# First batch of a spectral MLP kernel: filter rows, store queue and load order

## The chip, the cores and the metric

The kernel runs on one core of one Trainium2 chip. The metric is the device time of one execution in microseconds (us), the median of the runs shown. The engines are TensorE (PE, with its weight loads PEld), VectorE (DVE), ScalarE (ACT), GpSimd (POOL) and SyncE (SP), which here only issues DMAs; ACT can issue DMAs too. An engine takes its instructions in order, a DMA issue included.

## The reference

A batch of 4 sequences of 3136 tokens with 256 features goes through three parts. In the reference's words, cut:

```python
X = np.fft.rfft(x, axis=1)
y = np.fft.irfft(X * (filt_r + 1j * filt_i)[None], n=3136, axis=1)      # part 1: a filter per frequency and feature
u = y + np.real(np.fft.fft(np.fft.fft(y, axis=1), axis=2))              # part 2: mixing, then an MLP
x2 = u + np.maximum(layer_norm(u) @ w_ch1, 0) @ w_ch2
out = x2 + np.maximum(layer_norm(x2) * g_ln @ v_ch1, 0) @ v_ch2         # part 3: a second MLP
```

The weights are float64 and are handed to the kernel as pairs of 32-bit words; everything else is float32. The MLPs have 1024 hidden features.

## The kernel before, in words

The sequence length is 64 x 49, and a transform over it is done as one of length 64 (over p) and one of length 49 (over q), each a matrix product with a constant matrix.

For a batch b, `over_p(b)` loads x in 13 chunks (256 KB each, the last one 128 KB), multiplies each by the matrix `f1`, copies the product from PSUM to a buffer `gst` on ACT and stores it to the DRAM tensor `g` (tile `gd`). `over_q(b)` reloads g in 16 chunks with the axes exchanged (`gr`, 98 rows of 2 KB) and goes through 17 steps t. A step multiplies by `f2` (and by a turned copy `f2s`), multiplies the spectrum by a chunk of the filter (`fc`) on DVE, adds the two parts into y on POOL (line 423), multiplies y by `i1` two steps later, and stores the result to the DRAM tensor `v` (`vd`, 100 rows of 2 KB, issued by ACT). The filter input `ff` has 128 rows per frequency, of which rows 0 to 48 and 64 to 112 hold the filter and the other 30 are zero.

For batch 0 these products are single float32 ones; for later batches operands are split into a high and a low part. After batch 0's `over_q`, `prep_ticks(0)` mixes and normalises the first block, and the MLP steps (`w1_step`, `w2_step`) run until the end, with the stages of the next batches interleaved.

The weight words are loaded in chunks of 512 KB (`ww`) and converted to two float32r parts by `conv_ticks`: four DVE passes, two ACT passes, a multiplication on POOL and a split on ACT and POOL for each chunk. The conversion is a generator; each tick handles a different phase of up to four chunks. The first three chunks of the first weight have a generator of their own (`cv`, letter `a`).

The order of the work is written out by hand. The order in which the program emits instructions is the order on each engine. Tables say after which tick of which stage a tick of something else is emitted: `DURING` by the tick of `over_q(0)`, `P0` by the tick of `over_p(0)`, `AFTER` behind `over_q(0)`. The letters are `a` and `c` (conversion ticks), `k` (load of constants), `s` (split of constants), `x` (loads of x of batch 1), `f` (tick of `over_p(1)`) and `p` (tick of `prep_ticks(0)`). DMAs of SP and ACT use eight completion counters in turn: a DMA waits until the earlier one on the same counter has landed.

In the kernel before, SP's queue for batch 0 begins with the first constant, seven chunks of x, two chunks of words, six chunks of x, five further constants, the thirteen stores of g, and only then the first filter chunk, a constant, a chunk of words and the reloads of g:

```python
            (nc.sync if exact(k) else nc.scalar).dma_start(out=pairs(g_dram[b][k * 256:k * 256 + n * 128]), in_=st[:, :n])
```

Of the kernel before, what the change touches and what calls it, by code (L numbers as in the profile page):

```python
# [9 lines left out]
F32 = mybir.dt.float32  # L10
# [3 lines left out]
ACTF = mybir.ActivationFunctionType  # L14
# [4 lines left out]
B, S, D, H = 4, 3136, 256, 1024  # L19
# [14 lines left out]
NCONST = len(CN) * 128 + 2 + NK + D + 128  # L34
# [94 lines left out]
NA, LAG = 3, 3  # L129
N1 = 8  # L130
AHEAD, XW = 4, 7
WHEN = (-1, -1, 0, 1, 3, 3, 4, 5)
DURING = {0: 'aa', 2: 'a', 6: 'a', 14: 'k', 16: 'a', 30: 'cs', 33: 'x', 35: 'ff', 36: 'sf', 37: 'cc', 39: 'f', 40: 'f'}
P0 = {9: 'a'}
AFTER = "ppcfspfcppfpfppfpppc"
CONV = (0, 1, 3, 6, 9, 11, 12, 14, 15, 17, 19, 20, 21, 22, 23, 24, 25, 26, 27, 28)
P1 = (2, 3, 4, 5, 7, 8, 9, 10, 10)
# [11 lines left out]
def spectral_mlp_kernel(ctx: ExitStack, tc, x, ff, cst, w1a, w2a, gln, w1b, w2b, out):  # L149
    nc = tc.nc  # L150
# [7 lines left out]
    wp = pool("wp", 1)  # L158
# [7 lines left out]
    fp = pool("fp", 3)  # L166
    tp = pool("tp", 1)
    yp = pool("yp", 3)
    zp2 = pool("zp2", 3)
    stg = pool("stg", 3)  # L170
    up = pool("up", 3)
    xnp = pool("xnp", 5)
# [25 lines left out]
    g_sb = keep.tile([128, 2], F32, name="g_sb")  # L198
    zsl = {s: keep.tile([128, 2, B, 64], F32R, name=f"zsl{s}") for s in "hl"}
    alt = keep.tile([128, D], F32R, name="alt")  # L200
    zmid = keep.tile([128, 256], F32R, name="zmid")
# [36 lines left out]
    g_dram, v_dram, zt_of = {}, {}, {}  # L238
    x_raw, x_tile = {}, {}
    g_raw = {}  # L240
    f_sb, f_tile = {}, {}
# [5 lines left out]
    def load_x(b, c):  # L247
        if b > 1 or c > 9 or (c > 3 if b else c < 4):
            t = raw.tile([128, 2, D], F32, tag="raw", name="xr")
        else:  # L250
            if c % 2 == 0:
                x_tile[0] = up.tile([128, 4, D], F32, tag="u", name="xr")
            t = x_tile[0][:, c % 2 * 2:c % 2 * 2 + 2]
        n = blocks_of(c)
        nc.sync.dma_start(out=t[:, :n], in_=x[b, :, 2 * c:2 * c + n])
        x_raw[b, c] = t[:, :n]

    def pairs(t):
        return t.rearrange("(j p) d -> p j d", p=128)
# [3 lines left out]
    def load_g(b, c):  # L263
# [2 lines left out]
        nc.sync.dma_start(out=t[:98], in_=src)  # L266
        g_raw[b, c] = t[:98]

    def load_f(b, i, eng=nc.sync):
        k0, k1 = XCH[i]  # L270
        nk = k1 - k0
        if b == 0 and i > 2:
            if i < 5:
                t = up.tile([128, 4, D], F32, tag="u", name="fc").rearrange("p a d -> p (a d)")
            else:
                j = i - 5
                if j % 4 == 0:
                    f_tile[0] = wp.tile([128, 4096], F32, tag="w" + ("2a", "1b", "2b")[j // 4], name="fc")
                t = f_tile[0][:, j % 4 * 1024:j % 4 * 1024 + 1024]
            t = t.rearrange("p (a t d) -> p a t d", t=2, d=D)  # L280
            eng.dma_start(out=t[:, :nk], in_=ff[:, k0:k1])
            f_sb[b, i] = t[:, :, 0], t[:, :, 1]
        else:
            t = fp.tile([128, 2, 2, D], F32, tag="f", name="fc")
            eng.dma_start(out=t[:, :nk], in_=ff[:, k0:k1])
            f_sb[b, i] = t[:, :, 0], t[:, :, 1]
# [19 lines left out]
    def over_p(b):  # L306
        g_dram[b] = dram.tile([NJ * 128, D], F32, tag="g", name="gd")
        NC = 13
        for c in range(3):
            if (b, c) not in x_raw:  # L310
                load_x(b, c)
        yield

        def exact(c):
            return b == 0 or b == 1 and c < N1

        xs = {c: operand(exact(c), x_raw.pop((b, c))) for c in range(2)}
        yield
        done = []

        def store():
            k, n, ps = done.pop()
            if b == 0 and k % 5 > 2:
                st = vrp.tile([128, 2, D], F32, tag="vr", name="gst")
            elif b == 1 and exact(k):
                if k % 2:
                    st = tp.tile([128, 2, D], F32, tag="t2", name="gst")
                else:
                    st = hp.tile([128, 512], F32R, tag="hl", name="gst").bitcast(F32)
                    st = st.rearrange("p (a d) -> p a d", d=D)  # L330
            else:
                st = stg.tile([128, 2, D], F32, tag="st", name="gst")
            nc.scalar.activation(out=st[:, :n], in_=ps[:, :n], func=ACTF.Copy)  # L333
            (nc.sync if exact(k) else nc.scalar).dma_start(out=pairs(g_dram[b][k * 256:k * 256 + n * 128]), in_=st[:, :n])

        for c in range(NC):
            if c + 3 < NC and (b, c + 3) not in x_raw:
                load_x(b, c + 3)
            if b == 1 and c == N1:
                for i in range(c, c + 2):  # L340
                    xs[i] = operand(False, x_raw.pop((b, i)))
                yield
            if c + 2 < NC and not (b == 1 and N1 - 2 <= c < N1):
                xs[c + 2] = operand(exact(c + 2), x_raw.pop((b, c + 2)))
            n = blocks_of(c)
            ps = bank(2)
            product(exact(c), ps[:, :n].rearrange("p a d -> p (a d)"), "f1", xs.pop(c), 0, n * D)
            if done:
                store()
            done.append((c, n, ps))  # L350
            if b > 1 or c == NC - 1 or not exact(c + 1):
                store()
            yield

    def over_q(b):
# [4 lines left out]
        n = len(XCH)  # L360
# [18 lines left out]
        for c in range(3):  # L379
            load_g(b, c)  # L380
        if b == 0:
            for i in range(1, ahead):
                load_f(b, i)
        yield
        gs[0] = operand(b == 0, g_raw.pop((b, 0)))
# [103 lines left out]
    def load_v(U):  # L489
        ts = []  # L490
        for eo in range(2):
            t = vrp.tile([128, 2, D], F32, tag="vr", name="vr")
            r0 = 50 * 32 * eo
            if U < NU:
                r0 += 64 * (1 + U % 6 * 4)
                nc.sync.dma_start(out=t, in_=pairs(v_dram[U // 6][r0:r0 + 256]))
            else:
                for b in range(B):
                    h = 64 * (b % 2)
                    nc.sync.dma_start(out=t[h:h + 64, b // 2], in_=v_dram[b][r0:r0 + 64])  # L500
            ts.append(t)
        v_raw[U] = ts
# [211 lines left out]
    def run(it, k=None):  # L714

        while it and (k is None or k > 0):
            if next(it, StopIteration) is StopIteration:
                return False
            if k is not None:
                k -= 1  # L720
        return True

    with tc.manual_schedule():
        def load_consts(c0, c1):
            if c0 % 512 == 0:
                i = c0 // 512
                t = hp.tile([128, 512], F32R, tag="h" + "hhl"[i], name="cr").bitcast(F32)
                cf[i] = t
            t = cf[c0 // 512][:, c0 % 512:c0 % 512 + c1 - c0]
            nc.sync.dma_start(out=t, in_=cst[:, c0:c1])  # L730
            return t

        def consts():
            for i in (2, 1, 0):
                cs_done.add(i)
                split(cf[i], chi[:, i * 512:i * 512 + 512], clo[:, i * 512:i * 512 + 512],
                      nc.vector if i == 2 else nc.gpsimd)
                yield
# [9 lines left out]
        def bufs_b(kind, i):  # L748
# [9 lines left out]
                return flat(yp.tile([128, 2, D], F32, tag="y", name="wm"))  # L758
            return flat(zp2.tile([128, 2, D], F32, tag="z", name="we"))

        load_consts(0, 128)
        p0 = over_p(0)
        for c in range(XW):
            load_x(0, c)
        cv = conv_ticks(["1a"], bufs_a, lambda i: -1 if i < 2 else 1, 0, NA)
        run(cv, 1)
        for c in range(XW, 13):
            load_x(0, c)
        run(p0, 1)
        load_consts(128, 512)  # L770
        nc.sync.dma_start(out=ctail, in_=cst[:, nw - 128:nw - 128 + ctail.shape[1]])
        nc.sync.dma_start(out=g_sb, in_=gln)
        ar = zp2.tile([128, 2, D], F32, tag="z", name="ar")[:, 0]
        nc.sync.dma_start(out=ar, in_=cst[:, NCONST - D - 128:NCONST - 128])
        turned[0] = xnp.tile([128, D], F32, tag="xn", name="f2s")[:, :128]
        nc.sync.dma_start(out=turned[0], in_=cst[:, NCONST - 128:])
        cs = consts()
        q0 = over_q(0)
        k = 0
        while run(p0, 1):  # L780
            k += 1
            for what in P0.get(k, ""):
                run(cv, 1)
        load_f(0, 0)
        load_consts(512, 1024)
        for what in DURING.get(0, ""):
            run(cv, 1)
        nc.scalar.activation(out=alt, in_=ar, func=ACTF.Copy)
        nc.scalar.activation(out=zmid, in_=ar, func=ACTF.Copy, scale=0.0)
        p1 = over_p(1)  # L790
        act = {
            "a": lambda: run(cv, 1),
# [8 lines left out]
        k = 0  # L801
        while run(q0, 1):
            k += 1
            for what in DURING.get(k, ""):
                act[what]()
        load_v(0)
        p = prep_ticks(0)
        for what in AFTER:
            act[what]()
# [2 lines left out]
        nc_ = sum(v.count("c") for v in (*DURING.values(), AFTER))  # L812
        assert nf >= 2 + N1
        assert sum(v.count("s") for v in (*DURING.values(), AFTER)) == 3
        assert sum(v.count("a") for v in DURING.values()) + sum(map(len, P0.values())) >= NA + LAG


        blocks = [(0, 0)]
# [156 lines left out]
```

## Time and profile before

| what | value |
|---|---|
| median of 3 runs | 1425.43 us (1424.55 to 1427.17) |
| the profiled execution | 1426.04 us, its span 1424.3 us |
| PE busy | 1382.0 us, 97% of the span |
| DVE, ACT, POOL busy | 62%, 44%, 29% |
| DMA | 123.66 MB, 87 GB/s over the span |

The page gives shares over the whole span. They hide that the kernel has two parts: a beginning of some 160 us in which the engines wait for each other and for transfers, and the rest, in which PE has no pause. The views that show the beginning are the windows (busy time by stretch), the timeline of one engine, the chain of waits and the list of DMA issues.

### The profile page before, as it was taken

What the parts mean: (1) busy time and instruction counts of PE and PEld (TensorE: products, weight loads), DVE (VectorE), ACT (ScalarE), POOL (GpSimd) and SP (SyncE); (2) the same over time, 40 slices, a digit from 0 to 9 for tenths busy, and PEclk for the clock granted to TensorE, in tenths of its full rate; (3) what the DMA queues carried; (4) which work ended last, traced back from release to release, by engine and by line L of the source; (5) the groups of instructions that cost most, each with busy time, mean ns of one, the idle gap of its engine ahead of it and who ended that gap; (6) DMA issues with size and microseconds to landing.
All of it is one profiled execution on the core that took longest, in us unless ns stands there. A gap on an engine that the chain in (4) does not pass through costs nothing.

```text
span 1424.3 us, 22897 instructions
## 1 busy us (share of the span) xinstructions
PE 1382.0 (97%) x8835; PEld 1218.7 (86%) x8835; DVE 879.4 (62%) x1798; ACT 622.7 (44%) x1350; POOL 408.4 (29%) x361
## 2 busy tenths in 40 slices
PE   4968999999999999999999999999999999999998
PEld 2437899888989999898999998898999999999998
DVE  1779977777554765766544676667555555555453
ACT  4655545546444444545344355445333233323222
POOL 1636534544231333434032244334100010100000
PEclk7999999999999999999999999999999999999999
DMA  9983332422233313312233223131000000000000
GB/s 322 305 286 108 103 113 69 140 92 71 79 117 121 97 53 109 110 46 68 71 104 114 83 85 114 48 109 62 19 30 30 31 1 31 31 16 16 31 15 23
DMA packets 65981, 123.66 MB, mean 87 GB/s; under 512 B 6096, under 2 KB 32848, under 8 KB 65872
## 3 DMA queue, kind: packets, MB, share of 16 engines
q1 hardware_dynamic: 49920, 99.00, 21.3%
q10 hardware_dynamic: 15952, 23.20, 5.0%
q8 instruction: 69, 1.13, 0.3%
q14 instruction: 40, 0.33, 0.1%
HBM read 83.12 MB, written 39.06 MB: 86 GB/s over the span
## 4 chain that ended last, share of the span: by engine, by line
PE 90%; DMA 4%; DVE 3%; ACT 1%; issue 1%; POOL 1%; SPq 0%; ACTq 0%; POOLq 0%
PE ps L705 37%; PE ps L682 37%; PE ps L217 11%; PE ps L612 3%; DMA xr<-in_x 2%; PE ps L303 1%; DMA vd<-vst 1%; DMA fc<-in_ff 1%; PE ps L440 1%; DVE we L652 1%; ACT gst L333 0%; DVE wm L665 0%; DMA gd<-gst 0%; PE ps L550 0%; DVE hl L688 0%
## 5 line engine op out<-in xcount | busy, mean ns | idle before, releaser
L687 ACT ACTIVATE hh<-ps 128x512 fp32r<-128x512 f32 (+1 forms) x400 | 235.6, 589 | 686.5 <-PE ps L682 664.8
L688 DVE SCALAR_TENSOR_TENSOR hl<-ps,hh 128x512 fp32r<-128x512 f32 (+1 forms) x400 | 271.7, 679 | 426.1 <-ACT hh L687 425.0
L682 PE MATMUL ps<-xth,w1a 128*128 128x512 f32 (+1 forms) x800 | 245.6, 389 | 0.0
L682 PE MATMUL ps<-xth,w1b 128*128 128x512 f32 (+1 forms) x800 | 243.7, 386 | 0.0
L705 PE MATMUL ps<-w2a,hh 128*128 128x256 f32 x1568 | 221.3, 283 | 1.3 <-ACT hh L687 1.3
L705 PE MATMUL ps<-w2b,hh 128*128 128x256 f32 x1568 | 218.3, 281 | 0.0
L705 PEld LDWEIGHTS ps<-w2b,hh 128*128 128x128 f32 x1568 | 206.2, 188 | 10.5
L705 PEld LDWEIGHTS ps<-w2a,hh 128*128 128x128 f32 x1568 | 205.2, 189 | 10.3 <-ACT hh L687 2.0
L599 POOL TENSOR_TENSOR rs<-rs,mhalf 128x4 f32<-128x4 f32 (+1 forms) x51 | 50.4, 988 | 415.8 <-DVE rs L598 407.5
L682 PE MATMUL ps<-xtl,w1a 128*128 128x512 f32 (+1 forms) x400 | 155.9, 390 | 0.0
L682 PE MATMUL ps<-xtl,w1b 128*128 128x512 f32 (+1 forms) x400 | 155.7, 389 | 0.0
L682 PEld LDWEIGHTS ps<-xth,w1a 128*128 128x128 f32 x800 | 135.9, 189 | 17.8 <-ACT xth L220 0.5
L682 PEld LDWEIGHTS ps<-xth,w1b 128*128 128x128 f32 x800 | 135.1, 188 | 16.5
L705 PE MATMUL ps<-w2a,hl 128*128 128x256 f32 x784 | 122.9, 278 | 3.5 <-DVE hl L688 3.5
L705 PE MATMUL ps<-w2b,hl 128*128 128x256 f32 x784 | 121.9, 277 | 0.0
L423 POOL TENSOR_TENSOR y<-y,t 128x512 f32<-128x512 f32 (+1 forms) x67 | 87.0, 1299 | 101.6 <-DVE t L421 85.9
L705 PEld LDWEIGHTS ps<-w2a,hl 128*128 128x128 f32 x784 | 104.5, 188 | 4.1 <-DVE hl L688 4.1
L705 PEld LDWEIGHTS ps<-w2b,hl 128*128 128x128 f32 x784 | 103.8, 188 | 0.0
L221 POOL TENSOR_TENSOR sl<-gr,sh 98x512 fp32r<-98x512 f32 x48 | 63.3, 1319 | 109.5 <-ACT sh L220 109.5
L221 POOL TENSOR_TENSOR sl<-y,sh 128x512 fp32r<-128x512 f32 (+1 forms) x51 | 67.1, 1316 | 80.3 <-issue 59.4
L682 PEld LDWEIGHTS ps<-xtl,w1a 128*128 128x128 f32 x400 | 75.3, 188 | 14.9
L682 PEld LDWEIGHTS ps<-xtl,w1b 128*128 128x128 f32 x400 | 75.2, 188 | 14.4
(114 smaller groups left out, 2030.1 us busy)
## 6 DMA issues: line engine op xcount, KB each, us to landing
fc<-in_ff SPq DMA_DIRECT2D x61, 512.0 KB
vd<-vst ACTq DMA_DIRECT2D x64, 200.0 KB
gr<-gd SPq DMA_DIRECT2D x64, 196.0 KB
xr<-in_x SPq DMA_DIRECT2D x48, 256.0 KB
vr<-vd SPq DMA_DIRECT2D x48, 256.0 KB
out<-u SPq DMA_DIRECT2D x24, 512.0 KB
gd<-gst ACTq DMA_DIRECT2D x28, 256.0 KB
gd<-gst SPq DMA_DIRECT2D x20, 256.0 KB
```

The source lines that it names most:

```text
L217: nc.tensor.matmul(out=o, lhsT=lhs[a], rhs=rhs[b], start=start and i == 0, stop=stop and i == 2)
L221: (lo_eng or nc.vector).tensor_tensor(out=lo, in0=src, in1=f32(hi), op=ALU.subtract)
L303: nc.tensor.matmul(out=o, lhsT=cf[i // 512][:k, i % 512:i % 512 + w], rhs=rhs[:k, c0:c1], start=start, stop=stop)
L423: (nc.gpsimd if b or t < n - 1 else nc.vector).tensor_tensor(out=y[:, :nk], in0=y[:, :nk], in1=t2[:, :nk], op=ALU.add)
L440: nc.tensor.transpose(zp[:, a].rearrange("p t k -> p (t k)"), z[:, a], ident)
L599: nc.gpsimd.tensor_tensor(out=rs[:, tl], in0=rs[:, tl], in1=mhalf[:, tl], op=ALU.pow)
L612: nc.tensor.transpose(ps[:, t * 128:t * 128 + 128], xs[t][:, k * 128:k * 128 + 128], ident)
L652: nc.vector.scalar_tensor_tensor(out=p, in0=w[:, :, 1], scalar=-0x80000000, in1=p, op0=ALU.bitwise_and, op1=ALU.bitwise_or)
L682: nc.tensor.matmul(out=ps[:, :n], lhsT=w[:, a, k, m * 128:m * 128 + 128], rhs=xt[s][:, k, :n], start=i == 0, stop=i == 5)
L687: nc.scalar.activation(out=h[:, :n], in_=ps[:, :n], func=ACTF.Relu)
L688: nc.vector.scalar_tensor_tensor(out=l[:, :n], in0=ps[:, :n], scalar=0.0, in1=f32(h[:, :n]), op0=ALU.max, op1=ALU.subtract)
L705: nc.tensor.matmul(out=o[:, t % 2], lhsT=a[:, t * 128:t * 128 + 128], rhs=w[:, b, m], start=m == 0 and i == 0 and t % 2 == 0, stop=m == 7 ...
```

## The change

- The filter chunks of batch 0 are loaded in three DMAs each: rows 0 to 47, rows 64 to 111, and the two rows 48 and 112. Rows 32 to 63 and 96 to 127 of the place are cleared before, by POOL, or by DVE for the first two of the three large places. All large places are allocated at the beginning and each filter chunk keeps the place it had.
- The stores of g for batch 0 are issued by ACT, each behind its copy.
- The order on SP is now: first constant, all x, constants, filter chunks 0 and 1, a constant, the reloads of g, filter chunks 2 and 3, and then a chunk of words at a time. The conversion of the first three chunks of words runs wholly within `over_q(0)`. Two small inputs (`ar`, `gln`) are loaded at its eighth tick, and the two ACT copies of `ar` come after it.

The diff, cut to its core:

```diff
-DURING = {0: 'aa', 2: 'a', 6: 'a', 14: 'k', 16: 'a', 30: 'cs', 33: 'x', 35: 'ff', 36: 'sf', 37: 'cc', 39: 'f', 40: 'f'}
-P0 = {9: 'a'}
+DURING = {2: 'a', 7: 'a', 12: 'a', 15: 'a', 18: 'a', 19: 'k', 22: 'a', 26: 'a', 29: 'cs', 32: 'x', 34: 'ff', 35: 'sf', 36: 'cc', 38: 'f', 39: 'f'}
...
+    def rest(t, eng):
+        for r in (32, 96):
+            eng.memset(t[r:r + 32], 0.0)
+
+    def rows(t, src):
+        for r in (slice(0, 48), slice(64, 112), slice(48, 113, 64)):
+            nc.sync.dma_start(out=t[r], in_=src[r])
...
             if i < 5:
                 t = up.tile([128, 4, D], F32, tag="u", name="fc").rearrange("p a d -> p (a d)")
+                rest(t, nc.gpsimd)
             else:
                 j = i - 5
-                if j % 4 == 0:
-                    f_tile[0] = wp.tile([128, 4096], F32, tag="w" + ("2a", "1b", "2b")[j // 4], name="fc")
-                t = f_tile[0][:, j % 4 * 1024:j % 4 * 1024 + 1024]
+                t = f_tile[j // 4][:, j % 4 * 1024:j % 4 * 1024 + 1024]
             t = t.rearrange("p (a t d) -> p a t d", t=2, d=D)
-            eng.dma_start(out=t[:, :nk], in_=ff[:, k0:k1])
+            rows(t[:, :nk], ff[:, k0:k1])
+            f_sb[b, i] = t[:, :, 0], t[:, :, 1]
+        elif b == 0:
+            t = fp.tile([128, 2, 2, D], F32, tag="f", name="fc")
+            rest(t.rearrange("p a t d -> p (a t d)"), nc.gpsimd)
+            rows(t[:, :nk], ff[:, k0:k1])
             f_sb[b, i] = t[:, :, 0], t[:, :, 1]
...
-            (nc.sync if exact(k) else nc.scalar).dma_start(out=pairs(g_dram[b][k * 256:k * 256 + n * 128]), in_=st[:, :n])
+            (nc.sync if b and exact(k) else nc.scalar).dma_start(out=pairs(g_dram[b][k * 256:k * 256 + n * 128]), in_=st[:, :n])
...
-            for i in range(1, ahead):
+            for i in range(2, ahead):
                 load_f(b, i)
...
         load_consts(0, 128)
         p0 = over_p(0)
-        for c in range(XW):
+        for c in range(13):
             load_x(0, c)
-        cv = conv_ticks(["1a"], bufs_a, lambda i: -1 if i < 2 else 1, 0, NA)
-        run(cv, 1)
-        for c in range(XW, 13):
-            load_x(0, c)
+        for j, n in enumerate(("2a", "1b", "2b")):
+            f_tile[j] = wp.tile([128, 4096], F32, tag="w" + n, name="fc")
+            if j < 2:
+                rest(f_tile[j], nc.vector)
         run(p0, 1)
...
+        load_f(0, 0)
+        load_f(0, 1)
+        load_consts(512, 1024)
         cs = consts()
         q0 = over_q(0)
...
+        run(p0)
+        run(q0, 1)
+        rest(f_tile[2], nc.gpsimd)
+        cv = conv_ticks(["1a"], bufs_a, lambda i: i - 1, 0, NA)
...
         while run(q0, 1):
             k += 1
+            if k == 8:
+                ar = xnp.tile([128, D], F32, tag="xn", name="ar")
+                nc.sync.dma_start(out=ar, in_=cst[:, NCONST - D - 128:NCONST - 128])
+                nc.sync.dma_start(out=g_sb, in_=gln)
             for what in DURING.get(k, ""):
                 act[what]()
         load_v(0)
+        nc.scalar.activation(out=alt, in_=ar, func=ACTF.Copy)
+        nc.scalar.activation(out=zmid, in_=ar, func=ACTF.Copy, scale=0.0)
```

SP's queue between the loads of x and the reloads of g, before (`gst` are the copies to be stored to g, `cr` constants, `fc` filter chunks, `ww` weight words, `gr` reloads of g; line numbers are those of the kernel before):

```order
L334 DMA gd<-gst 128x2x256 x12
L334 DMA gd<-gst 128x256
L285 DMA fc<-in_ff 128x1024
L730 DMA cr<-in_cst 128x512
L637 DMA ww<-in_w1a 128x1024
L266 DMA gr<-gd 98x512 x3
L285 DMA fc<-in_ff 128x512
L285 DMA fc<-in_ff 128x1024
```

The same place now, up to the fourth reload of g (line numbers of the changed kernel; `f2s` is the turned matrix):

```order
L786 DMA f2s<-in_cst 128x128
L275 DMA fc<-in_ff 48x1024 x2
L275 DMA fc<-in_ff 2x1024
L275 DMA fc<-in_ff 48x512 x2
L275 DMA fc<-in_ff 2x512
L742 DMA cr<-in_cst 128x512
L265 DMA gr<-gd 98x512 x3
```

The thirteen stores have left SP's queue, and the reloads of g stand behind the first two filter chunks and a constant; the chunk of words comes after filter chunk 3, three filter DMAs for each chunk.

POOL's queue from its first work to the first additions y of the stage over q, before:

```order
L203 MEMSET mhalf 128x4
L654 ISA
L654 TENSOR_TENSOR we<-we 128x512
L221 TENSOR_TENSOR w1a<-we,w1a 128x512
L654 TENSOR_TENSOR we<-we 128x512
L423 TENSOR_TENSOR y<-y,t_284 128x512
L423 TENSOR_TENSOR y<-y,t_295 128x256
```

And now:

```order
L202 MEMSET mhalf 128x4
L271 MEMSET fc 32x1024 x8
L271 MEMSET fc 32x4096 x2
L435 ISA
L435 TENSOR_TENSOR y<-y,t_270 128x512
L271 MEMSET fc 32x1024 x2
L435 TENSOR_TENSOR y<-y,t_287 128x256
```

Ten clears stand before the first addition, and the two clears of filter chunk 4 (the fifth) between the first and the second.

## Rows read from the trace of the kernel before

**Rows 1.** Windows: each engine's busy time (instructions), granted clock, DMA share, GB/s.
```profile
core 0: us, PE busy (x) PEld busy (x) DVE busy (x) ACT busy (x) POOL busy (x), PEclk, DMA share, GB/s
0.00:10.00 10.00, 5.77 (x7) 2.49 (x8) 0.00 (x0) 2.75 (x4) 0.30 (x5) 1.00 0.76 255
10.00:20.00 10.00, 7.95 (x20) 3.42 (x18) 2.82 (x6) 3.49 (x7) 0.00 (x0) 1.00 1.06 374
20.00:30.00 10.00, 0.00 (x0) 0.00 (x0) 0.69 (x1) 6.70 (x14) 1.47 (x2) 0.50 1.01 334
...
50.00:60.00 10.00, 10.00 (x30) 4.50 (x29) 7.25 (x12) 7.44 (x22) 5.58 (x4) 1.00 0.89 282
60.00:70.00 10.00, 10.00 (x29) 4.52 (x28) 6.33 (x11) 7.62 (x24) 5.75 (x4) 1.00 0.98 349
70.00:80.00 10.00, 9.41 (x26) 3.91 (x25) 5.61 (x10) 6.64 (x20) 4.32 (x3) 1.00 0.93 324
...
110.00:160.00 50.00, 45.04 (x276) 39.45 (x275) 45.78 (x76) 29.27 (x59) 28.89 (x23) 0.97 0.33 111
160.00:1424.00 1264.00, 1257.95 (x8350) 1141.61 (x8347) 771.41 (x1614) 531.92 (x1139) 339.81 (x302) 1.00 0.21 67
```

**Rows 2.** Timeline of PE: start, duration, instruction, [idle before, what ended it].
```profile
4.23 13.71 PE L303 MATMUL ps<-xr,cr 128*128 128x512 f32 x26 [4.23 <-DMA xr<-in_x]
32.39 4.60 PE L303 MATMUL ps<-gr,cr 98*128 98x256 f32 x8 [14.45 <-DMA fc<-in_ff]
...
41.74 1.02 PE L303 MATMUL ps<-gr,cr 98*128 98x512 f32 x2
...
78.45 1.02 PE L409 MATMUL ps<-gr,f2s 98*128 98x512 f32 x2
...
107.52 1.63 PE L682 MATMUL ps<-xth,w1a 128*128 128x512 f32 x2
```

**Rows 3.** Timeline of ACT, 0 to 46 us.
```profile
17.89 5.04 ACT L333 ACTIVATE gst<-ps 128x512 f32<-128x512 f32 x8 [5.75 <-DMA gd<-gst]
...
24.90 0.40 ACT L788 ACTIVATE alt<-ar 128x256 fp32r<-128x256 f32 x1
```

**Rows 4.** The chain of waits: start, duration, what it went through.
```profile
14.78 3.00 DMA gd<-gst
...
23.06 3.08 DMA gd<-gst
...
26.27 0.38 SPq L266
...
101.63 2.32 DMA xr<-in_x
```

**Rows 5.** Waits of SP, 0 to 150 us: in total, times, longest.
```profile
SPq L334 <- ACT gst L333: 18.8, 13, 5.6
```

**Rows 6.** Timeline of SP: the issue of one filter load.
```profile
38.37 0.37 SPq L281 DMA_DIRECT2D fc<-in_ff  x1
```

**Rows 7.** Timeline of POOL: the first additions of the stage over q.
```profile
36.65 2.05 POOL L423 TENSOR_TENSOR y<-y,t 128x512 f32<-128x512 f32 x2 [1.66 <-DVE t L421]
```

**Rows 8.** POOL by line and shape: count, busy us, mean ns.
```profile
L423 POOL TENSOR_TENSOR y<-y,t 128x512 f32<-128x512 f32 x63 | 83.9, 1332 | 101.2 <-DVE t L421 85.9 <-DVE t L419 10.5 <-ACT fc L369 4.6
...
L534 POOL CAST zmid<-zsh 1x256 fp32r<-1x256 f32 x24 | 10.5, 437 | 151.2 <-ACT zsh L518 151.2
...
L203 POOL MEMSET mhalf<- 128x4 f32 x1 | 0.1, 101 | 0.3 <-POOLq L944 0.3
```

**Rows 9.** DMA issues of the first 100 us: count, size of each.
```profile
fc<-in_ff SPq DMA_DIRECT2D x16, 512.0 KB
...
vd<-vst ACTq DMA_DIRECT2D x16, 200.0 KB
gr<-gd SPq DMA_DIRECT2D x16, 196.0 KB
```

**Rows 10.** DVE by line and shape, 0 to 90 us: the longest pass of a conversion.
```profile
L666 DVE SCALAR_TENSOR_TENSOR we<-ww,we 128x512 f32<-128x512 uint32 x5 | 3.5, 693 | 0.2
```

More of the change, by code (lines that the diff above doesn't have):

```diff
@@ L771, in spectral_mlp_kernel @@
         nc.sync.dma_start(out=ctail, in_=cst[:, nw - 128:nw - 128 + ctail.shape[1]])
-        nc.sync.dma_start(out=g_sb, in_=gln)
-        ar = zp2.tile([128, 2, D], F32, tag="z", name="ar")[:, 0]
-        nc.sync.dma_start(out=ar, in_=cst[:, NCONST - D - 128:NCONST - 128])
         turned[0] = xnp.tile([128, D], F32, tag="xn", name="f2s")[:, :128]
         nc.sync.dma_start(out=turned[0], in_=cst[:, NCONST - 128:])
+        load_f(0, 0)
+        load_f(0, 1)
+        load_consts(512, 1024)
         cs = consts()
         q0 = over_q(0)
[L779 to L789, printed above, removed]
+        run(p0)
+        run(q0, 1)
+        rest(f_tile[2], nc.gpsimd)
+        cv = conv_ticks(["1a"], bufs_a, lambda i: i - 1, 0, NA)
         p1 = over_p(1)
@@ L814, in spectral_mlp_kernel @@
         assert sum(v.count("s") for v in (*DURING.values(), AFTER)) == 3
-        assert sum(v.count("a") for v in DURING.values()) + sum(map(len, P0.values())) >= NA + LAG
+        assert sum(v.count("a") for v in DURING.values()) >= NA + LAG
         blocks = [(0, 0)]
```

## The prediction

> **What bounds the kernel now.** Read the windows first [rows 1]. From 160 us to the end TensorE (PE) is busy for 1257.95 of 1264 us, and the order of the work there is the same before and after. So whatever the change does, it does before 160 us, and a start that comes earlier by so much ends the kernel earlier by so much. In the stretch 110 to 160 us VectorE (DVE) is busy for 45.78 of 50 us with conversions and layer norms that follow the first stages in a fixed order; it moves as a block with them.
>
> In the first 80 us two things run near their limit. The DMA engines are 0.89 to 1.06 busy in the windows shown between 10 and 80 us and move 282 to 374 GB/s; PE is full from 50 to 70 us, and only there at 10.00 [rows 1]. Before that it stands still: the thirteen first products (the stage over p) end at 4.23 + 13.71 = 17.94 us, and the first product of the next stage (over q) starts at 32.39 us after an idle time of 14.45 us [rows 2]. [...]
>
> Why the hole? The chain of waits gives three pieces [rows 4]. ScalarE (ACT) idles 5.75 us before its last eight copies [rows 3], because the stores that free its buffers stand on SyncE (SP) behind all loads of x, two chunks of weight words and five constants: the first store is issued at 14.78 us. The last store goes out at 23.06 and lands 3.08 us later. The reload of g follows at 26.27, behind a filter, a constant and a chunk of words, and the stage begins at 32.39, 6.1 us later. On its side SP spent 18.8 us waiting for these copies [rows 5].
>
> **The change, part by part.**
>
> Stores on ACT: thirteen stores leave the SP queue and are issued after each copy on ACT. ACT needs 5.04/8 = 0.63 us per copy [rows 3], PE 0.86 us per tile at full clock, so a store issue fits beside. PE's stage was never starved of x (26 pieces in one run [rows 2]), so it still ends near 17.9. Copy 0.6 and landing 3.1 put the last store at 21.6 at the earliest. The other bound is bytes: x and g are 3.28 MB each, the constants 0.41, the two first filters 0.60, together 7.6 MB; 2.55 MB go in the first 10 us and the rest at 374 GB/s [rows 1] takes until 23.4. I take 22.0, nearer the first, since not all of the filters and constants must be through. The reload now has nothing in front of it: between 2.32 us (the shortest landing in the chain) and the 6.1 us of before [rows 4]. I take 2.5, because the queue ahead is empty. The stage over q then starts at **24.5 instead of 32.4: 7.9 us earlier**; 3 to 9 are the ends.
>
> Clearing: ten clears of 32x1024 go to POOL, two of 32x4096 to POOL, four of 32x4096 to DVE. The trace has only tiny clears, 0.10 us for 4 elements [rows 8]. The nearest row is POOL's copy of 256 elements, (437-101)/256 = 1.3 ns an element; the upper bound is its two-input add, (1332-101)/512 = 2.4 ns. I take the copy's, which like a clear does no arithmetic: 1.45 us for 1024 and 5.5 us for 4096. Six clears then end at 10 us. The fourth filter's wait for the x tile that they reuse, near 11.5 us; two more, and the two long ones, end at 25.4. DVE is idle until the stage over q [rows 1], so its four cost nothing even at 5 us each.
>
> But the fifth filter (i=4) is cleared on POOL behind the first add y of the stage. That add came 36.65-32.39 = 4.26 us after the stage's start [rows 2, 7], so now near 28.8. Add 1.3, two clears 2.9, three filter loads and the g reload behind them on SP at 0.37 each [rows 6] = 1.5, landing 2.3: step t=4 can start at 36.8. Before, it started at 41.74 [rows 2]. Of the 7.9 us **4.9 remain**; this wait is new, since SP is held at that filter and g's fourth reload stands behind it.
>
> Filter loads without zero rows: 98 of 128 rows, so each 524 KB load becomes 401 KB; over 33 frequencies 2.03 MB go, 6.3 us at 324 GB/s. It is no gain by itself while PE is full; it pays for the words. Three chunks of words (524 KB each) formerly went mostly before the stage and now go inside it, two of them after t=4. From there on 12 filters, 12 reloads, 16 stores of 205 KB, two chunks and 0.4 MB of constants make 11.9 MB [rows 9], which at PE's 13 steps of 2.8 us asks for 328 GB/s; the windows show 282 to 349. I charge **0.5 us** (0 to 3). SP issues five instead of three for a step's loads and waits; 1.6 us out of 2.8 is room. All DMAs take eight completion counters in turn, so 8 outstanding DMAs now cover 1.6 steps and not 2.7; that is in the 0 to 3.
>
> Words converted a chunk at a time: each has four DVE passes of at most 0.69 us [rows 10] and some ACT and POOL work, formerly in the hole, now between steps. In 60 to 70 us DVE has 3.7, ACT 2.4 and POOL 4.2 us free out of 10 [rows 1]; three chunks over 48 us fit, with two steps of buffering to absorb a late one. Nothing charged (0 to 2).
>
> The two small copies of the alternating row move from the hole to the end of the stage on ACT, ahead of the copies that the first mixing waits for: 2 x 0.40 less overlap [rows 3] = **0.7 us**. The stage's tail (78.45 to the first w1 product at 107.52 [rows 2]) keeps its 29 us; with fewer bytes queued ahead of the next batch's x I take **0.5 off** (0 to 2).
>
> Sum: -4.9 + 0.5 + 0.7 - 0.5 = -4.2 us on the profiled execution of 1426.04 us (span 1424.3): 1421.8. That execution is 0.6 above the median of 1425.43, so **1421.2**.
>
> **Rivals.**
>
> *The filter parts run at half rate* (ends slower). Every transfer to SBUF in the first 100 us touches at least 98 rows [rows 9]; a 48-row part has no row of its own. If one went at half of 374 GB/s, a filter would take 401/187 = 2.14 us in place of 1.40. With reload and store (406 KB, 1.09 us) a step needs 3.23 us of DMA against PE's 2.80: +0.43 x 13 = 5.6, the words and constants (1.44 MB, 3.9 us) find no gap, and t=4 loses another 0.7. -4.9+5.6+3.9+0.7+0.7 = +6: 1431.4. It decides once a part falls below about 284 GB/s. For it: engines already 0.9 busy. Against: 98-row reloads and 100-row stores share windows of 349 GB/s. Chance 0.17.
>
> [...]
>
> *POOL clears slowly* at the add's 2.4 ns: the long clears end at 36.4, the first add waits for them, t=4 comes at 46.6, 4.9 late, and the result is 1431. Break-even is near 2.0 ns. Chance 0.08.
>
> *The transfers set the end anyway*: two new gaps, waiting for the last store (2.5 us) and for the fifth filter (3.5 us), cost the 6.3 us that the bytes save; 1425. Chance 0.17. For it: DMA share [rows 1].
>
> *The fifth filter isn't late* (its clear or g's reload hidden): the 7.9 stays, about 1418.5. Chance 0.13.
>
> **How the numbers follow.** My own case has 0.45, between 1419 and 1424. About 0.2% (2.85 us) can be told from no change: faster means below 1422.6. The forecast's better part, the larger gain and some of the rest give 0.57; same 0.20; slower 0.23 (both slow rivals below zero, less a part of them). The range takes in the larger gain and most of the half-rate case: 1416.5 to 1430.5.
>
> **What would show it.** The first product over q near 24 to 25 us, ACT without the 5.75 us wait, the hole under 8 us; a PE wait of 2 to 3 us at the fourth or fifth step ended by g or a filter; filters landing in 2 to 4 us; steps of 2.8 to 3.0 us from there; the first w1 product near 103. A clear on POOL above 2 us, or steps of 3.2 us under full DMA, would make it wrong.

## The result, and the profile after

The changed kernel takes 1441.95 us (median of 4 runs, 1435.72 to 1446.12) against 1425.04 for the kernel before beside it: a ratio of 1.0113 [1.0089, 1.0137] (95% interval), 16.9 us slower by the medians. The prediction was 1421.2 us, in the range 1416.5 to 1430.5, so both the sign and the range were missed. The profiled execution took 1442.59 us with a span of 1440.8 us; the one before 1426.04 and 1424.3.

First the windows of the changed kernel (columns as in [rows 1]):

```profile
core 0: us, PE busy (x) PEld busy (x) DVE busy (x) ACT busy (x) POOL busy (x), PEclk, DMA share, GB/s
10.00:20.00 10.00, 7.51 (x19) 3.23 (x17) 6.94 (x2) 4.27 (x8) 7.86 (x4) 1.00 1.05 366
20.00:30.00 10.00, 1.06 (x3) 0.91 (x4) 0.00 (x0) 2.90 (x6) 1.04 (x1) 0.63 0.73 224
...
50.00:60.00 10.00, 6.89 (x15) 2.67 (x14) 5.10 (x7) 5.21 (x14) 3.17 (x3) 0.84 0.83 221
60.00:70.00 10.00, 8.20 (x23) 3.48 (x22) 8.54 (x14) 7.28 (x21) 6.09 (x5) 0.99 0.75 213
70.00:80.00 10.00, 7.51 (x18) 3.07 (x17) 6.49 (x8) 4.77 (x14) 6.79 (x5) 0.86 0.82 237
```

Compare 60 to 80 us with [rows 1]. There the DMA engines were 0.98 and 0.93 busy and moved 349 and 324 GB/s; now they are 0.75 and 0.82 busy and move 213 and 237. The busy share fell by a fifth, the bytes by a third: a busy DMA engine moves less than before. PE, which had been full from 50 to 70 us, now pauses.

The timeline of PE shows the pauses (start, duration, instruction, [idle before, what ended it]; t is the step of the stage over q, and t=4 is the product at 41.77):

```profile
4.12 13.40 PE L315 MATMUL ps<-xr,cr 128*128 128x512 f32 x26 [4.12 <-DMA xr<-in_x]
28.94 4.35 PE L315 MATMUL ps<-gr,cr 98*128 98x256 f32 x8 [11.42 <-DMA gr<-gd]
...
41.77 1.10 PE L315 MATMUL ps<-gr,cr 98*128 98x512 f32 x2 [2.56 <-DMA gr<-gd]
...
55.67 1.10 PE L315 MATMUL ps<-gr,cr 98*128 98x512 f32 x2 [3.10 <-DMA gr<-gd]
56.60 1.71 PE L421 MATMUL ps<-gr,f2s 98*128 98x512 f32 x2
58.11 1.92 PE L315 MATMUL ps<-y,cr 128*100 128x512 f32 x2
...
76.82 1.59 PE L315 MATMUL ps<-gr,cr 98*128 98x512 f32 x2 [2.31 <-DMA gr<-gd]
...
91.84 1.02 PE L421 MATMUL ps<-gr,f2s 98*128 98x512 f32 x2
...
121.28 1.84 PE L694 MATMUL ps<-xth,w1a 128*128 128x512 f32 x2
```

Against [rows 2]: the stage over q starts 3.45 us earlier (28.94 for 32.39). At step t=4 that lead is gone (41.77 for 41.74). At t=16 the kernel is 13.4 us late (91.84 for 78.45) and at the first w1 product 13.8 (121.28 for 107.52). The two profiled executions are 16.6 us apart, so all but some 2.8 us is lost before that product, nearly all of it between t=4 and t=16, and every long pause of PE there ends with a reload of g. The clock falls with the pauses: two of the three windows from 50 to 80 us have a granted clock of 0.84 and 0.86, and behind the pause of 3.10 us two pairs of products take 1.71 and 1.92 us where such a pair takes 1.02 at the full clock. How much of that lengthens the stage, in which PE waits for reloads again later, wasn't separated.

The waits of SP, 0 to 150 us (in total, times, longest), show what the late reloads stand behind:

```profile
SPq L275 <- DMA vd<-vst: 10.6, 3, 4.6
SPq L265 <- DMA vd<-vst: 7.3, 5, 3.4
SPq L275 <- DMA fc<-in_ff: 6.0, 8, 1.5
```

Line 275 issues a filter part, line 265 a reload of g. A filter part has nothing to do with a store of v; what it shares with it is a completion counter (the trace has eight for all DMAs of SP and ACT). These three rows hold 24 us of SP's time behind earlier transfers that haven't landed. By themselves such waits don't tell the kernels apart: over its stage, up to t=16, SP waits 26.5 us in all behind transfers here, 25.2 in the kernel before, and 31.8 in one_full below, which isn't slow. The chain of waits (start, duration, what) goes through such transfers one after another:

```profile
22.45 3.61 DMA gd<-gst
26.27 2.53 DMA gr<-gd
...
37.56 4.07 DMA gr<-gd
...
46.53 4.16 DMA vd<-vst
53.92 7.05 DMA ww<-in_w1a
...
68.79 3.87 DMA vd<-vst
72.72 3.96 DMA gr<-gd
```

A chunk of words takes 7.05 us to land, and a store or a reload of 0.2 MB around 4. (The chain of one_full has landings as long, 6.99 us for words and 6.19 for a store.)

The last 2.8 us come behind the first w1 product, where the work is the same. Windows of 20 us, counted from that product, in the kernel before (from 107.52) and after (from 121.28):

```profile
107.52:127.52 20.00, 18.85 (x114) 15.99 (x113) 18.27 (x25) 12.60 (x26) 14.64 (x11) 0.97 0.35 119
...
167.52:187.52 20.00, 17.51 (x119) 15.84 (x119) 18.97 (x36) 10.19 (x20) 11.70 (x9) 1.00 0.30 97
```

```profile
121.28:141.28 20.00, 18.78 (x108) 15.94 (x107) 17.46 (x23) 12.44 (x25) 14.55 (x11) 0.91 0.35 118
...
181.28:201.28 20.00, 17.50 (x106) 15.44 (x106) 19.46 (x35) 9.45 (x18) 10.92 (x9) 0.91 0.20 60
```

PE is busy for the same 18.8 and 17.5 us, but the granted clock is 0.91 in both windows where it was 0.97 and 1.00. By estimate that is 20 x (0.06 + 0.09) = 3.0 us less work done. The mean granted clock of the whole span also differs between the changed kernel's four executions: 0.991 in the fastest (1435.72 us), 0.985 or 0.986 in the other three (1441.32 to 1446.12). The one with the trace is one of these three.

### The profile page after: what moved, and what is told of

Same layout as the page of the kernel before. It is cut to its first block, busy times and chain, and to the rows that moved or that the text cites. A ratio compares the mean times of both kernels' runs of the same rounds, so it can differ in the third digit from the quotient of the medians.

```text
span 1440.8 us, 22991 instructions
## 1 busy us (share of the span) xinstructions
PE 1392.0 (97%) x8835; PEld 1223.4 (85%) x8835; DVE 897.0 (62%) x1802; ACT 621.8 (43%) x1350; POOL 425.6 (30%) x373
## 4 chain that ended last, share of the span: by engine, by line
PE 90%; DMA 4%; DVE 3%; issue 1%; ACT 1%; POOL 0%; SPq 0%; ACTq 0%; DVEq 0%; POOLq 0%
PE ps L717 37%; PE ps L694 37%; PE ps L216 11%; PE ps L624 3%; PE ps L315 1%; DMA vd<-vst 1%; PE ps L452 1%; DMA gr<-gd 1%; DMA xr<-in_x 1%; DVE we L664 1%; DMA gd<-gst 1%; DMA ww<-in_w1a 0%; DVE wm L677 0%; PE ps L562 0%; DVE hl L700 0%
## 5 line engine op out<-in xcount | busy, mean ns | idle before, releaser
L694 PEld LDWEIGHTS ps<-xth,w1a 128*128 128x128 f32 x800 | 136.9, 190 | 18.1 <-ACT xth L219 0.5
L694 PEld LDWEIGHTS ps<-xtl,w1b 128*128 128x128 f32 x400 | 75.5, 189 | 14.5
```

Source lines behind the costliest of these rows:

```text
L694: nc.tensor.matmul(out=ps[:, :n], lhsT=w[:, a, k, m * 128:m * 128 + 128], rhs=xt[s][:, k, :n], start=i == 0, stop=i == 5)
```

## The experiments

| label | what runs | median us | ratio to before |
|---|---|---|---|
| one_full | the change, each filter chunk whole in one DMA, no clears | 1425.88 | 1.0005 [0.9995, 1.0015] |
| three_full | the same in three DMAs by columns | 1432.82 | 1.0052 [1.0032, 1.0072] |
| no_two_rows | the change without the two-row DMA (leaves out rows 48 and 112 of the filter) | 1437.22 | 1.0083 [1.0064, 1.0103] |
| before_split | before, with the split filter loads and the clears alone | 1438.78 | 1.0099 [1.0079, 1.0119] |
| two_row_halves | the change, rows 0 to 63 and 64 to 127 in two DMAs, no clears | 1446.11 | 1.0136 [1.0112, 1.016] |
| two_col_halves | the same bytes in two DMAs by columns | 1427.0 | 1.0008 [0.9996, 1.0019] |
| before_act_stores | before, with the stores of g on ACT alone | 1429.34 | 1.0017 [1.0007, 1.0028] |
| full_clears | the change, each chunk whole in one DMA, clears kept | 1428.72 | 1.0019 [1.001, 1.0029] |
| stores_shared | one_full, the last seven stores on SP | 1425.81 | 0.9997 [0.9986, 1.0009] |
| stores_shared_early | that, with a filter chunk and words ahead of the last stores | 1428.66 | 1.0023 [1.0011, 1.0034] |
| probe | before, with 96 filter chunks loaded ahead in eight forms, one execution | 1702.64 | (rates, no comparison) |

### Which part loses: the loads, the clears, or the order?

**one_full** undoes part 1 of the change and keeps the order and the stores on ACT:

```diff
-        for r in (32, 96):
-            eng.memset(t[r:r + 32], 0.0)
+        return
...
-        for r in (slice(0, 48), slice(64, 112), slice(48, 113, 64)):
-            nc.sync.dma_start(out=t[r], in_=src[r])
+        nc.sync.dma_start(out=t, in_=src)
```

> The changed kernel, but each filter chunk of batch 0 in one DMA of all 128 rows, without clears; stores on ACT and load order as changed. Theory C (counters): the three DMAs of a filter chunk use up the eight completion counters, and SP waits for landings; with one DMA the steps over q come back to 2.8 to 3.0 us, 1418 to 1426 us. Theory H (half rate of 48-row parts): the same, 1418 to 1426. Theory W (words inside the stage over q hold DVE and the transfers): it stays near the changed kernel, above 1433.

**before_split** is the opposite: the kernel before with part 1 alone (`rest`, `rows` and the kept places, as in the diff of the change).

> The kernel before with the first part of the change alone: filter chunks of batch 0 in three DMAs of 48, 48 and 2 rows, large places kept and cleared; stores on SP and words first, as before. Theories C and H: slower than before, 1432 to 1445 us, steps over q of 3.2 us and more. Theory W: within 3 us of before (1422 to 1428).

Measured: without part 1 the kernel is level with before (1.0005), and part 1 alone makes the kernel before 13.6 us slower. The loss is part 1's; order and stores together are worth nothing either way.

**full_clears** tells clears from loads: the clears stay, each chunk is one whole DMA.

```diff
-        for r in (slice(0, 48), slice(64, 112), slice(48, 113, 64)):
-            nc.sync.dma_start(out=t[r], in_=src[r])
+        nc.sync.dma_start(out=t, in_=src)
```

> The changed kernel with whole filter chunks in one DMA of 128 rows, but the clears kept (one_full with clears). It prices the clears and the wait of the fifth filter chunk for its clear on POOL. The prediction's working: the fourth step (t=4) about 3 us later than in one_full; if nothing takes it back 1427 to 1430 us. The rival: the clears are hidden, within 1 us of one_full (1425.9).

Measured: 1428.72, which is 2.8 us above one_full by the medians (2.0 by the ratios, whose intervals overlap a little) and 13.2 below the change. PE's timeline of one_full and then of full_clears:

```profile
27.95 4.43 PE L313 MATMUL ps<-gr,cr 98*128 98x256 f32 x8 [10.76 <-issue]
...
37.59 1.10 PE L313 MATMUL ps<-gr,cr 98*128 98x512 f32 x2
...
77.72 1.02 PE L419 MATMUL ps<-gr,f2s 98*128 98x512 f32 x2
...
106.09 1.55 PE L692 MATMUL ps<-xth,w1a 128*128 128x512 f32 x2
```

```profile
29.35 4.21 PE L314 MATMUL ps<-gr,cr 98*128 98x256 f32 x8 [11.65 <-issue]
...
41.96 1.10 PE L314 MATMUL ps<-gr,cr 98*128 98x512 f32 x2 [2.35 <-DMA gr<-gd]
```

From the start of the stage to t=4 one_full needs 9.64 us, full_clears 12.61, the changed kernel 12.83. The 3 us between are the fifth filter's wait for its clear; the shape of the loads adds only 0.2 us before t=4. Behind t=4 the times part: full_clears reaches t=16 at 80.92, the change at 91.84.

### What about the loads: rows, or the number of DMAs?

**three_full** has three DMAs for a chunk, as the change, but each over all 128 rows, and all bytes:

```diff
-        for r in (slice(0, 48), slice(64, 112), slice(48, 113, 64)):
-            nc.sync.dma_start(out=t[r], in_=src[r])
...
+        parts = ((slice(0, 1), slice(0, 2)), (slice(1, 2), slice(0, 1)), (slice(1, 2), slice(1, 2)))
...
+        for p in parts:
+            nc.sync.dma_start(out=t[(slice(0, 128),) + p], in_=src[(slice(0, 128),) + p])
```

(A chunk of one frequency is cut in three in the same way; no clears.)

> As one_full, but each filter chunk in three DMAs of all 128 rows and a part of the columns (512, 256, 256), so that no part has few rows and the number of DMAs is that of the change; 512 KB a chunk. Theory C: as slow as the change or slower, 1438 to 1452 us, DMA share below 0.85 in the stage over q. Theory H: as one_full within 3 us. Theory W: above 1433, like one_full.

**no_two_rows** drops the third, small DMA (`for r in (slice(0, 48), slice(64, 112))`). It leaves two rows of the filter out, so only its time is of use.

> The changed kernel without the third DMA of a filter chunk: rows 48 and 112 of the filter are left out (they hold zeros from the clears). Theory C: four DMAs a step instead of five, so about half of the loss comes back: 1428 to 1436 us. Theory H: nothing changes, within 3 us of the change, 1438 to 1445. A theory that the two-row DMA itself is slow (T): nearly all of the loss comes back, below 1428.

Measured: three whole-row DMAs cost 6.9 us over one. Dropping the two-row DMA gives 4.7 us by the medians, but the intervals of no_two_rows and the change overlap, so that is not shown. The number of DMAs has a price of its own, but three_full, with a third more bytes than the change, is still 9.1 us faster than it: neither theory C (1438 or more) nor theory H (within 3 us of one_full) holds alone. To cut this cleanly, the next pair has the same bytes and the same number of DMAs and differs only in how a chunk is cut, into 64 rows of 4 KB or into 128 rows of 2 KB:

```diff
-        for r in (slice(0, 48), slice(64, 112), slice(48, 113, 64)):
+        for r in (slice(0, 64), slice(64, 128)):
             nc.sync.dma_start(out=t[r], in_=src[r])
```

> The changed kernel with each filter chunk of batch 0 in two DMAs of 64 rows (0 to 63, 64 to 127), all 128 rows, no clears: 512 KB in two DMAs. Theory H: the parts go at half rate, 1434 to 1445 us. Theory C: as two_col_halves within 3 us, 1427 to 1432.

```diff
+        n = t.shape[1]
+        for a in range(2):
+            p = (slice(0, 128), slice(a, a + 1)) if n == 2 else (slice(0, 128), slice(0, 1), slice(a, a + 1))
+            nc.sync.dma_start(out=t[p], in_=src[p])
```

> As two_row_halves, but the two DMAs have all 128 rows and half of the columns each: the same bytes and the same number of DMAs. Both theories: between one_full (1426) and three_full (1433), 1427 to 1432 us.

Measured: 1446.11 against 1427.0, so 19 us for the cut by rows (1.1 us above theory H's range; theory C, within 3 us of each other, falls). The column halves have the shorter pieces and are the faster, so the length of a piece isn't the cause. The window from 30 to 80 us of the first and of the second:

```profile
30.00:80.00 50.00, 36.67 (x79) 16.32 (x78) 28.92 (x46) 20.87 (x61) 18.50 (x14) 0.78 0.92 210
```

```profile
30.00:80.00 50.00, 44.90 (x123) 19.97 (x122) 41.81 (x64) 34.08 (x98) 30.20 (x22) 0.98 0.98 321
```

Nearly the same busy share, 210 GB/s against 321.

**probe** measures the rates by themselves: in the kernel before, ahead of everything, eight stretches of twelve chunk loads each into the three large places, with clears between that part the stretches:

```diff
+        for cuts in (
+            ((slice(0, 128), al),),
+            ((slice(0, 48), al), (slice(64, 112), al)),
+            ((slice(0, 48), al), (slice(64, 112), al), (slice(48, 113, 64), al)),
+            ((slice(0, 48), al),),
+            ((slice(0, 64), al), (slice(64, 128), al)),
+            ((slice(0, 128), slice(0, 512)), (slice(0, 128), slice(512, 1024))),
+            ((slice(0, 98), al),),
...
+        ):
+            for t in reversed(pt):
+                nc.vector.memset(t, 0.0)
+            for j in range(12):
+                parts(j, *cuts)
```

> The kernel before, with eight stretches of filter loads put ahead of it, twelve chunks each into the same three large places, a clear of the places on DVE between the stretches: whole chunks of 128 rows; 48 and 48 rows; 48, 48 and 2 rows; 48 rows of the lower half alone; 64 and 64 rows; 128 rows in two halves of the columns; 98 rows; 112 rows. Nothing else runs, so each stretch's bytes over its time is a rate. Theory H (half rate of parts within one half of the rows): whole chunks at 330 to 390 GB/s, 48+48 at 170 to 230, the lower half alone the same or lower, 64+64 at 170 to 230, the column halves as whole chunks. Theory C (counters and number of DMAs alone): 48+48 within 15% of whole chunks, 64+64 and the column halves alike; the 2-row parts cost under 5%.

Windows of the stretches in the order of the diff (the last two columns are DMA share and GB/s):

```profile
13.70:32.40 18.70, 0.00 (x0) 0.00 (x0) 0.00 (x0) 0.00 (x0) 0.00 (x0) 1.00 0.87 336
44.40:72.60 28.20, 0.00 (x0) 0.00 (x0) 0.06 (x1) 0.00 (x0) 0.00 (x0) 1.00 0.90 167
84.70:111.20 26.50, 0.00 (x0) 0.00 (x0) 0.02 (x1) 0.00 (x0) 0.00 (x0) 1.00 0.81 182
123.20:141.30 18.10, 0.00 (x0) 0.00 (x0) 0.03 (x2) 0.00 (x0) 0.00 (x0) 1.00 0.83 131
153.30:183.00 29.70, 0.00 (x0) 0.00 (x0) 0.00 (x0) 0.00 (x0) 0.00 (x0) 1.00 0.90 212
195.00:216.20 21.20, 0.00 (x0) 0.00 (x0) 0.07 (x2) 0.00 (x0) 0.00 (x0) 1.00 0.85 297
228.20:248.00 19.80, 0.00 (x0) 0.00 (x0) 0.01 (x1) 0.00 (x0) 0.00 (x0) 1.00 0.76 243
```

Twelve whole chunks take 18.7 us, 1.56 each, at 336 GB/s. The change's three parts take 26.5 us, 2.21 each: a quarter fewer bytes, 42% more time. The two-row part isn't what costs here, since the two 48-row parts alone take 28.2 us. That they take longer than with it (26.5) is not explained; each stretch was timed once. One part of 48 rows takes 18.1 us, nearly as long as all 128 rows. Halves by rows take 29.7 us and halves by columns 21.2, with the same bytes and the same number of DMAs. Two parts of 64 rows carry a third more bytes than two of 48 in nearly the same time (29.7 and 28.2 us, or 26.5 with the two rows). So the 16 rows left out of each half save some 5 to 11% of the time, not 25%. The eighth stretch (112 rows) ran into the kernel's own loads of x and can't be read.

Two parts of 48 rows took 28.2 us where twice the lower one alone would be 2 x 18.1 = 36.2, a gain in rate of 28% (167 against 131 GB/s). Why a part of 48 or 64 rows goes at a lower rate, no run shows.

### Why did the earlier start bring nothing?

**before_act_stores** moves only the stores:

```diff
-            (nc.sync if exact(k) else nc.scalar).dma_start(out=pairs(g_dram[b][k * 256:k * 256 + n * 128]), in_=st[:, :n])
+            (nc.sync if b and exact(k) else nc.scalar).dma_start(out=pairs(g_dram[b][k * 256:k * 256 + n * 128]), in_=st[:, :n])
```

> The kernel before with the second part of the change alone: the stores of g for batch 0 on ACT; whole filter chunks, words first. If the stores behind SP's queue cost the start of the stage over q, it starts 3 to 5 us earlier than 32.4 us. If nothing takes that back, 1420 to 1423 us; if the transfers set the end of the stage, within 1.5 us of before.

Measured: 1.0017, 2.5 us slower, which neither expectation had. SP's timeline there:

```profile
7.88 8.21 SPq L255 DMA_DIRECT2D xr<-in_x  x6
...
31.96 1.22 SPq L266 DMA_DIRECT2D gr<-gd  x3
```

Six loads of x stretch over 8.21 us, where the kernel before takes 4.50 for them and SP's issue alone is 0.37 each [rows 6], and the first reload goes out at 31.96 us instead of 26.27 [rows 4]. The stage over q starts at 34.66. So moving the stores alone doesn't bring the stage forward; the new order alone was not run. In the changed kernel ACT's timeline shows how far the two together do:

```profile
21.00 0.60 ACT L345 ACTIVATE gst<-ps 128x512 f32<-128x512 f32 x1 [0.50 <-ACT gst L345]
21.63 0.37 ACTq L346 DMA_DIRECT2D gd<-gst  x1
22.04 0.38 ACT L345 ACTIVATE gst<-ps 128x256 f32<-128x256 f32 x1 [0.44 <-ACT gst L345]
22.45 0.34 ACTq L346 DMA_DIRECT2D gd<-gst  x1
```

A copy (0.60 us) and a store issue (0.37) go one after the other, 1.04 us for a tile, more than PE's 0.86. The stage over p, done on PE at 17.52 us, ends on ACT at 22.79.

**stores_shared** has ACT issue the first six stores and SP, free by then, the last seven; **stores_shared_early** also puts a filter chunk and the first words ahead of SP's stores:

```diff
-            (nc.sync if b and exact(k) else nc.scalar).dma_start(out=pairs(g_dram[b][k * 256:k * 256 + n * 128]), in_=st[:, :n])
+            (nc.sync if exact(k) and (b or k > 5) else nc.scalar).dma_start(out=pairs(g_dram[b][k * 256:k * 256 + n * 128]), in_=st[:, :n])
```

> one_full with the first six stores of g on ACT and the last seven on SP, whose queue is free of x by then. On ACT a copy and its store issue take 1.04 us, more than PE's 0.86 us a tile; on SP the issues run beside the copies. If the stores set the start of the stage over q, its first product comes 2 to 4 us before that of one_full (27.95); 1422 to 1425 us if some of it is kept, within 1 us of one_full if the transfers in the stage over q take it back.

```diff
...
+        run(p0, 7)
+        load_f(0, 2)
+        cv = conv_ticks(["1a"], bufs_a, lambda i: i - 1, 0, NA)
+        run(cv, 1)
         run(p0)
...
```

> stores_shared, with filter chunk 2 and the first chunk of words ahead of the last stores on SP, in the stretch where SP otherwise waits for the stores to land. If the idle transfers of 20 to 30 us (DMA share 0.78 in one_full) are worth it, 1 to 3 us below stores_shared; if the larger queue ahead of the last stores costs as much, the same within 1 us.

Measured: 0.9997 and 1.0023. The first starts the stage at 28.65 us, no earlier than one_full's 27.95; the second at 32.45, where the kernel before starts it, and ends 2.9 us behind the first. The expected 2 to 4 us from a lighter ACT did not come: with the last seven stores off ACT, its copies wait for an earlier store to land and free the buffer. ACT and PE of stores_shared:

```profile
21.96 1.07 ACT L343 ACTIVATE gst<-ps 128x512 f32<-128x512 f32 x2 [3.67 <-DMA gd<-gst]
```

```profile
28.65 4.42 PE L313 MATMUL ps<-gr,cr 98*128 98x256 f32 x8 [11.17 <-issue]
```

No form of the order tried beats the kernel before measurably.

Where one_full's 4.4 us went is in its PE times: at t=16 it leads by 0.7 us (77.72 for 78.45), at the first w1 product by 1.4 (106.09 for 107.52). Windows of the stage from its first product to t=16, one_full and then the kernel before:

```profile
27.95:77.72 49.77, 45.31 (x122) 20.54 (x122) 40.54 (x62) 32.99 (x95) 29.54 (x22) 0.96 0.97 327
```

```profile
32.39:78.45 46.06, 44.62 (x122) 20.47 (x123) 32.67 (x53) 30.52 (x90) 25.30 (x19) 0.95 0.95 314
```

The stage of one_full moves 327 x 49.77 = 16.3 MB, that of the kernel before 14.5, with the DMA engines nearly full in both: the words that formerly went in the hole now go here. The lead was time in which bytes moved.

## Why the prediction was wrong, by its own steps

**The filter loads: the step that failed.** They were charged 0.5 us (0 to 3), from a byte count at full rate: 401 instead of 524 KB for a load. Measured, a load takes 2.21 us instead of 1.56 (probe), and the stretch from t=4 to t=16 grew by 13.3 us (91.84 - 42.70 = 49.1, before 78.45 - 42.60 = 35.9, product of line 421 or 409 each time). full_clears, which differs in the loads alone, grew by 2.2 there (80.92 - 42.90 = 38.0); the other 11.1 us are the loads, with the pauses and the lower clock that they bring. The trace of before had no row of a 48-row transfer, the text said so, and still put its value at the byte count's end.

**The half-rate rival (chance 0.17) was the outcome** in kind; its 1431.4 us is still 10.6 below the measured time. That a part goes at half of 374 GB/s was an estimate, and no row of the kernel before showed it; in the probe the three parts went at 182 GB/s and whole chunks at 336. The evidence I held against it was weak: 98-row reloads sharing windows of 349 GB/s. A window's mean over a mix says nothing of the rate of one shape; alone, 98 rows go at 243 GB/s. Its price fell short too: 2.14 us for a filter was close to 2.21, but the step of 3.23 us came out as 49.1/12 = 4.1. It took the DMA engines as the only limit, while they are 0.75 to 0.83 busy from 50 to 80 us; SP also stands waiting on counters, and three DMAs instead of one cost 6.9 us (three_full). Why the number of DMAs costs that stays open: in the stage of three_full SP waits 24.7 us behind transfers (28 to 85 us), not more than in one_full.

**The start of the stage over q**: 24.5 us predicted, 28.94 measured. PE ended at 17.5 as said (17.9), and the reload took 2.53 (2.5). What failed is "a store issue fits beside": I set ACT's 0.63 us against PE's 0.86 and left out the 0.37 us of the issue. With the waits of the middle tiles (one copy is done at 13.19 us and its store goes out at 14.47) the last store went out at 22.45 and landed 3.61 us later, at 26.06 for a predicted 22.0. That is not the whole of it: stores_shared took seven issues off ACT and its stage started at 28.65 us all the same. The other bound, by bytes, which the prediction set at 23.4 us and passed over for the earlier one, was the nearer of the two.

**The fifth filter's clear**: right in kind, and in size by luck. From the stage's start to t=4 I had 12.3 us, and it was 12.83; but the two clears took 1.94 us for 2.9, the issues 1.0 for 1.5, and the reload landed in 4.07 for 2.3, so the errors nearly cancel. As the start was 4.4 us late, t=4 came at 41.77 for a predicted 36.8, and the 4.9 us of gain were none.

**The clears' prices** were too high, which cost the sum nothing. The changed kernel, by line and shape (count, busy us, mean ns, then idle before):

```profile
L271 DVE MEMSET fc<- 32x4096 f32 x4 | 13.9, 3472 | 4.4 <-issue 2.7 <-PEq L956 1.6
L271 POOL MEMSET fc<- 32x1024 f32 x10 | 9.4, 944 | 5.7 <-PE ps L315 5.2
L271 POOL MEMSET fc<- 32x4096 f32 x2 | 7.0, 3507 | 0.1
```

0.94 us and 3.51 on POOL where I took 1.45 and 5.5; 3.47 on DVE, within the 5. (Four clears in a row on DVE start 4.38 us apart, so one holds the engine for longer than its row says; that too is within the 5.) The rival of slow clears falls. One sum is slightly off: with the whole 7.9 us kept, the prediction's own terms give 1418.2, not 1418.5.

**Words, conversion and tail.** In one_full the stretch from t=4 to t=16 takes 77.72 - 38.52 = 39.2 us, 3.3 more than before: with the words moved inside it, it costs a little more than the upper end of 3. So the 0.5 us were too few even for whole loads: one_full leads by 4.15 us at t=4 (37.59 for 41.74) and by 0.7 at t=16, and the 4.9 would not have come through. From t=16 to the first w1 product it is 29.4 us in the changed kernel and 28.4 in one_full, against 29.1 before, so +0.7 and -0.5 together were about right; the two small copies stand on the changed kernel's chain with 0.30 us each at 102.21.

**Not in the sum at all**: the granted clock behind the first w1 product, worth 2.8 us in the profiled executions.

**"The transfers set the end anyway" (0.17)** names what the rest of the change shows: without part 1, order and stores give 1.0005, with the DMA engines 0.97 busy. Its own sum, two gaps against the bytes saved, isn't tested there, since one_full saves no bytes.

## What to carry to other kernels

Before rows are cut out of a load to save bytes, measure the load in its new shape: here two 48-row parts ran at half the rate of the whole 128 rows (167 against 336 GB/s), and with the two-row part a quarter fewer bytes took 42% more time. A high DMA busy share isn't a full rate (0.90 busy at 167 GB/s, 0.87 at 336, in the probe); read it with the GB/s beside it. And where transfers fill the stretch anyway (0.97 busy in one_full), a stage that starts earlier gains only what it does without moving more bytes into that stretch: of 4.4 us at the start one_full kept 0.7 at t=16.

## What the runs showed of the hardware that I had not expected

- Leaving out rows 48 to 63 of each half saves little of the time of a load (28.2, or 26.5 with the two rows, against 29.7 us for twelve), and the DMA share shows none of it: 0.90 in both stretches, and 0.87 for whole chunks at twice the bytes per second.
- Cutting a whole-row load in two by columns is nearly free in the kernel (1427.0 against 1425.88 us; 21.2 against 18.7 us for twelve loads alone), cutting it in three is not (1432.82).
- The granted clock after the same pause differs between kernels. Around 60 us behind the first w1 product PE idles twice for 1.2 to 1.3 us in both kernels; before, the clock stayed at 1.00 over that window, after it averaged 0.91, with a four-product group at 186.58 taking 1.22 us against 0.74 before.
- POOL is no slower at clearing than DVE. Their rows for 32x4096 are 3.51 and 3.47 us, but clears that follow one another start 3.54 us apart on POOL and 4.38 on DVE (4.28 in the probe, with 128 rows of 4096), which is 0.87 and 1.07 (1.04) ns for each of the 4096 elements of a row. The row of a DVE clear is shorter than what it costs.
